# Three moves of small work in a fused attention and feed-forward kernel: a weight rounding, a square, and a group's last SiLU

## The chip, the cores and the metric

The kernel runs on one core of one Trainium2 chip. The metric is the device time of one execution in microseconds. TensorE (PE) does the matrix products, ScalarE (ACT) activations and copies, VectorE (DVE) elementwise work and reductions, GpSimd (POOL) elementwise work, and SyncE (SP) issues nearly all DMAs in program order.

## The reference, cut to what matters

Eight batches of twelve heads, 448 positions, head width 64. q and k are RMS-normalised, attention is a plain softmax, and its output, with heads side by side (3584 tokens of 768), goes through two matrix products with a SiLU between them. All is float32.

```python
scores = scale * np.matmul(rmsnorm(q, g_q), rmsnorm(k, g_k).transpose(0, 1, 3, 2))
attn = softmax(scores)                     # the scores' maximum is taken off first
x = np.matmul(attn, v)                     # -> (3584, 768)
h = x @ w_in                               # (768, 2048)
out = (h * (1.0 / (1.0 + np.exp(-h)))) @ w_out
```

The first three lines are shortened in notation, not in what they compute.

## The kernel before

**Couples and groups.** Attention is done in 24 couples of four heads, c = 0 to 23. Six couples (`GROUP`) are two batches. The first product of the feed-forward part, x @ w_in, is done for two batches at a time as eight blocks of seven products each (a Strassen scheme, class `Seven`), so the blocks of batches 0 and 1 run while couples 6 to 11 are attended, and so on. After the last couple the remaining blocks and the second product follow alone.

**A couple's two stretches.** `visit(c)` is the attention of couple c: pairs of score products go into the two PSUM buffers named `sc` (L749), ACT takes their exponentials (L754), and products with v add up in the two banks `av` (L786). `between(c)` runs the feed-forward products (L955, banks `mm` and `sc`) in two halves, by `fill`, which deals other small work among PE's steps, one piece after so many steps. What a piece issues goes into each engine's queue at that point of the program. The whole order is thus written out by hand: there is no scheduler, and each engine works its queue in order.

**The one-column write.** A visit first completes the sums of couple c-1 with its leftover keys. PE adds to the two `av` banks, and between two parts of that a single column of one bank is written by another engine (`turn`, L762: ACT up to couple 6, DVE at that place after it). PE's next product into that bank waits for it.

**The squares of q.** For couples up to 6, `normalise(c + 1)` gives pieces; piece 0 squares half of the next couple's q on ACT (L474) and reduces on DVE (L475). In visits 1 to 5 it is called by `run_all(beside[0:1])` ahead of the leftover products and of `turn`.

**Rounding of w_in.** The weights arrive as float64 words and are turned into float32 by pieces of 128x512: `open` is two ACT instructions (L103, L104), `round` three on DVE (L126, L129, L133) and an integer add on POOL (L137), and then issues the next loads (L88). Letters say where this is done: "o" opens, "r" rounds the next piece, in `halves` by half couple (index 2(c-6)+half) and in `visits` by visit; the first letter of a visit is done right behind its first scores.

```python
    halves = {0: "ro", 1: "ro", 2: "ro", 3: "oro", 4: "or", 5: "or", 6: "or", 7: "oroo"}
    visits = {GROUP + 2: "rr", GROUP + 4: "rr"}
```

**The SiLU.** `halves_in` runs the eight blocks of a group. A block's two finished rows of 128x896 are `owed`: their SiLU on ACT (L1102) and their save to `hidden` on SP (L994) are issued when the next block has finished its first product. The rows come from a ring of three (`staged`), so a block's second row is the row that the block before filled first; the copy of product 5 (L975) writes it. The last block of a group has no next one, and its rows are activated at once, at the end of couples 11, 17 and 23. ACT needs another function table for SiLU than for the exponential, and the kernel asks for the exponential's table ahead of each visit by a one-element activation (L1638).

**Later in a half.** The second half of a couple also holds, for couples from 7 on: the reciprocals of the row sums (L833), the transposition of the next k (L685) and its gain (ACT L691), the square of the q after next (L698), its reduction (L704) and a small product of that (L715), which is the last of PE's work ahead of the next visit.

Of the kernel before, what the change touches and what calls it, by code (L numbers as in the profile page):

```python
# [542 lines left out]
def bounded(  # L543
# [4 lines left out]
    HW, HF = z.NW // 2, z.NF // 2  # L548
# [5 lines left out]
    NC, loads, place, norm, spare, ones, first, squares = (  # L554
        own[name] for name in ("NC", "loads", "place", "norm", "spare", "ones", "first", "squares")
    )
    GROUP, LATE = z.NPAIR, z.LATE
# [12 lines left out]
    work = mem.tile([P, 16 * S + z.NK], F32, name="work")  # L570
    at = 0

    def piece(n):
        nonlocal at
        at += n
        return work[:, at - n : at]
# [5 lines left out]
    r = [piece(S) for _ in range(2)]  # L582
# [13 lines left out]
    for i, words in enumerate(late):  # L596
        m = len(pieces) - 4 + i
# [161 lines left out]
    def turn(step, copy):  # L759

        if step != weighed["step"]:
            copy(banks[1][:, S : S + 1], minus_half)  # L762
# [226 lines left out]
    def staged():  # L989
        stages.append(stages.pop(0))  # L990
        return stages[-1]

    def save(f, column, t):
        nc.sync.dma_start(hidden[f, :, ds(column, t.shape[1])], t)  # L994
# [11 lines left out]
    def fetch_ahead(group, m):  # L1006
        rows = [staged(), extra_stage if m else staged()]
        nc.sync.dma_start(rows[0], ahead[m])
        return rows, part_in(group, m, rows)
# [22 lines left out]
    def sum_x(group, c, steps=range(4)):  # L1032
        right_sums(*quarters(group, c), *sums_of_x(c), steps)

    def part_in(group, m, rows, prompt=False):

        chunk = 2 * m // room.CHUNK
        assert room.w_in.rounded >= (chunk + 1) * z.NW
        s = room.sums(chunk).rearrange("p (s c m k) -> p s c m k", s=3, c=HW, m=2)[:, :, :, m % 2]
        lefts = {  # L1040
            "1": lambda c: room.w1(c, 2 * m),
            "2": lambda c: room.w1(c + HW, 2 * m),
            "3": lambda c: s[:, 2, c],
            "4": lambda c: room.w1(c + HW, 2 * m + 1),
            "5": lambda c: s[:, 0, c],
            "6": lambda c: s[:, 1, c],
            "7": lambda c: room.w1(c, 2 * m + 1),
        }

        def right(name, c):  # L1050
            b11, b12, b21, b22 = quarters(group, c)
            t1, t2, t4 = sums_of_x(c)
            return {"1": b11, "2": b21, "3": b22, "4": t4, "5": t1, "6": t2, "7": b12}[name]

        def left(name, c):
            step = {"5": 0, "6": 1, "7": 2, "3": 3}.get(name)
            assert step is None or (chunk, step) in summed
            return lefts[name](c)

        done = {(i + 1, j + 1): rows[i][:, ts(j, S)] for i in range(2) for j in range(2)}  # L1060
        return Seven(left, right, range(HW), S, done, prompt)

    def halves_in(group, blocks, beside=lambda m: iter(()), begun={}, fetched=()):

        owed, ready = [], {}

        def prepare(m):
            if m in begun:
                return begun[m]
            if m in fetched:  # L1070
                return fetch_ahead(group, m)
            rows = [staged() for _ in range(2)]
            return rows, part_in(group, m, rows)

        for i, m in enumerate(blocks):
            rows, part = ready.pop(m) if m in ready else prepare(m)
            columns = part.five()
            if m not in begun and m not in fetched:
                columns = chain(part.two(), columns)
            aside = beside(m)  # L1080
            count = 0
            for n in columns:
                if n == 0:
                    yield n
                    continue
                count += 1
                if (count - 1) % HW == 0:
                    if count > HW:
                        activate(owed)
                    if count > 2 * HW and i + 1 < len(blocks) and blocks[i + 1] in fetched:  # L1090
                        if blocks[i + 1] not in ready:
                            ready[blocks[i + 1]] = prepare(blocks[i + 1])
                    next(aside, None)
                yield n
            for _ in aside:
                pass
            owed = [(2 * m + k, group[0], rows[k]) for k in range(2)]
        activate(owed)

    def activate(owed):  # L1100
        for f, b, t in owed:
            nc.scalar.activation(t, t, AF.Silu)  # L1102
            save(f, b * S, t)
        owed.clear()
# [144 lines left out]
    owed = []  # L1249
# [188 lines left out]


    step_of = {"o": lambda: room.w_in.open(), "r": lambda: room.w_in.round()}  # L1440
    halves = {0: "ro", 1: "ro", 2: "ro", 3: "oro", 4: "or", 5: "or", 6: "or", 7: "oroo"}
    visits = {GROUP + 2: "rr", GROUP + 4: "rr"}
    for c in range(GROUP // 2):
        halves[2 * (c - GROUP)], halves[2 * (c - GROUP) + 1] = "rr", "o"
    halves[-2], halves[-1] = "r", ""
# [21 lines left out]
    def last_two(c):  # L1467
        return [c // GROUP * 2 - 2, c // GROUP * 2 - 1]

    def visit(c):  # L1470

        beside = normalise(c + 1) if 0 < c <= GROUP else []
        if c == GROUP:
            beside = [lambda: None] + beside[2:]
        if c < NC:
            scores(c, 0, 0)
        for step in visits.get(c, "")[:1]:
            step_of[step]()
        if c == 0:
            first_q(1)  # L1480
            normalise_alone(1)
            scores(c, 1, 0)
        run_all(beside[0:1])
        if c > 0:
            weigh(c - 1, LEFT)
            weigh(c - 1, LEFT - 1, 0)
            turn(1, nc.scalar.copy if c <= GROUP else nc.vector.tensor_copy)
            if GROUP < c < NC and c % GROUP == 0:
                sum_x(last_two(c), 0, range(2, 4))
        if c < NC:  # L1490
            scores(c, 0, 1)
        if c > 0:
            weigh(c - 1, LEFT - 1, 1)
            if c - 1 < EARLY:
                for i in range(2):
                    nc.vector.tensor_copy(x_of(c - 1, i), sums[i])
                run_all(beside[1:2])
                if c == GROUP // 2 + 1:
                    divide(c - 2, None)
                if inverting:  # L1500
                    while len(inverting) > 1:
                        inverting.pop(0)()
                    if c > 1:
                        divide(c - 2, None)
            else:
                divide(c - 1, sums)
                if c == GROUP:
                    for i in range(1, HW):
                        sum_x(last_two(c), i, range(2))
                    for i in range(2):  # L1510
                        norm.scale(c + 1, q_of(c + 1), q_of(c + 1), i, nc.vector)
                    room.w_in.round()
                run_all(beside[1:2])
                if GROUP < c < NC and c % GROUP == 0:
                    for i in range(1, HW):
                        sum_x(last_two(c), i)
                weights_in_visit(c)
            if c + 1 < NC:
                loads["vrest"](c + 1)
        if c == NC:  # L1520
            return
        if c > 0:
            scores(c, 1, 0)
        scores(c, 1, 1)
        if c <= GROUP:
            run_all(beside[2:3])
        weigh(c, 0, 1)
        scores(c, 2, 0)
        weigh(c, 1, 1)
        turn(0, nc.scalar.copy)  # L1530
        if c < GROUP:
            run_all(beside[3:4])
        scores(c, 2, 1)
        weigh(c, 0, 0)
        if c < GROUP:
            scores(c, LEFT)
        if c != GROUP - 1:
            run_all(add(c, 1))
        weigh(c, 1, 0)
        if c < GROUP // 2:  # L1540
            room.w_in.open()
        if c >= GROUP:
            scores(c, LEFT)
        if c + 1 < NC:
            loads["v"](c + 1)
        if len(inverting) == 1:
            inverting.pop()()

    def run_all(work):
        for piece in work:  # L1550
            piece()

    def between(c):
# [36 lines left out]
        if c >= GROUP and c % GROUP == 0:  # L1590
            fetched = range(AHEAD) if c == GROUP else ()
            columns = products - 2 * HW * S * len(fetched)
            work = halves_in(last_two(c), range(HF), plain_in, dict(begun), fetched)
            begin(work, columns, 2 * GROUP)
            begun.clear()
        late = add(c, LEFT - 1) if c >= GROUP else []
# [46 lines left out]
    begun, inverting = {}, []  # L1643
# [23 lines left out]
    group = [z.B - 2, z.B - 1]  # L1667
# [219 lines left out]
```

## Time and profile before

| | us |
|---|---|
| median of 3 runs | 1303.18 (1303.07 to 1303.73) |
| the profiled execution's own time | 1303.14 |
| its span, first to last instruction | 1301.3 |
| PE busy in the span | 1289.3 |
| DVE busy | 955.8 |
| ACT busy | 503.7 |
| POOL busy | 357.1 |

The profile has one execution. Its parts are: busy time by engine, waits by pair of engine and releaser, and a timeline by engine with start, length, instruction and, in brackets, the idle time before it and what ended that. PE's matmuls are pipelined and their ends are modelled, so a late PE is read from its starts: a group of float32 products of 448 columns starts every 0.376 us when nothing holds it (two such groups, written x8 for the 64-row products, take 0.75 us). A visit's stretch from its first score product to the first feed-forward product behind it takes 10.97 us from 345.14 to 356.11, in couple 13.

### The profile page before, as it was taken

How to read it: one execution, taken by the hardware profiler on the slowest of the kernel's cores; microseconds unless marked ns; L12 is line 12 of the kernel's file. 1: busy time of each engine (PE TensorE's matmuls, PEld its weight loads, DVE VectorE, ACT ScalarE, POOL GpSimd, SP SyncE). 2: the span in 40 equal slices, each digit the busy share in tenths (PEclk: the TensorE clock that was granted, in tenths of full speed). 3: DMA queues.
4: the chain of work that ended last, by engine and by line, in shares of the span. 5: the costliest groups of instructions: out<-in, count | busy, mean ns of one | idle time of the engine just before them, and what ended most of it. 6: DMA issues, size and time to landing. Idle time of an engine off the chain costs nothing.

```text
span 1301.3 us, 19847 instructions
## 1 busy us (share of the span) xinstructions
PE 1289.3 (99%) x7182; PEld 831.3 (64%) x7182; DVE 955.8 (73%) x1650; ACT 503.7 (39%) x880; POOL 357.1 (27%) x221
## 2 busy tenths in 40 slices
PE   9999999999999999999999999999999999999998
PEld 4444444444444444444444455559999999999998
DVE  6998778868655557656554786698978787878785
ACT  7867566645554545544543344310000010000000
POOL 6755453443334334333311343400000000000000
PEclk9999999999999999999999999999999999999999
DMA  9674446434333444344321467312322223131411
GB/s 234 171 193 134 107 123 165 121 91 123 90 90 90 121 93 121 90 91 90 89 69 41 161 189 239 117 61 85 105 89 92 90 89 122 57 129 51 140 39 40
DMA packets 266159, 144.14 MB, mean 111 GB/s; under 512 B 203748, under 2 KB 249956, under 8 KB 266052
## 3 DMA queue, kind: packets, MB, share of 16 engines
q1 hardware_dynamic: 265424, 141.68, 39.5%
q8 instruction: 59, 0.97, 0.3%
q0 software_dynamic: 320, 0.90, 0.2%
q14 instruction: 48, 0.39, 0.1%
q10 hardware_dynamic: 308, 0.20, 0.1%
HBM read 95.36 MB, written 41.29 MB: 105 GB/s over the span
## 4 chain that ended last, share of the span: by engine, by line
PE 94%; ACT 2%; DVE 2%; issue 1%; DMA 0%; SPq 0%; POOL 0%; ACTq 0%; DVEq 0%; POOLq 0%
PE alone L1271 23%; PE mm L955 19%; PE sc L955 11%; PE av L786 10%; PE sc L749 10%; PE mm L1271 8%; PE alone L955 7%; PE alone L1309 2%; PE sc L824 1%; PE mm L824 1%; PE mm L1309 1%; PE sc L642 1%; PE sc L673 0%; DMA rows<-in_k_dram 0%; ACT work L754 0%
## 5 line engine op out<-in xcount | busy, mean ns | idle before, releaser
L754 ACT ACTIVATE work<-sc,rms 128x448 f32<-128x448 f32 x318 | 181.5, 634 | 74.2 <-PE sc L749 64.5
L749 PE MATMUL sc<-work 64*64 64x448 f32 x1344 | 164.3, 543 | 2.1 <-ACT work L754 0.9
L800 DVE TENSOR_TENSOR work<-work 128x896 f32<-128x896 f32 (+1 forms) x110 | 117.7, 1099 | 51.4 <-PE av L786 50.9
L786 PE MATMUL av<-work,rows 64*64 64x448 f32 x1272 | 151.3, 541 | 0.8 <-ACT av L762 0.5
L955 PE MATMUL mm<-x,W 128*128 128x448 f32 x366 | 150.2, 543 | 0.2 <-DVE stage L904 0.2
L955 PE MATMUL mm<-sums_x,W 128*128 128x448 f32 x348 | 143.2, 543 | 0.9 <-DVE stage L904 0.9
L503 POOL TENSOR_TENSOR rms<-rms,minus_half 128x14 f32<-128x14 f32 (+4 forms) x40 | 96.4, 2413 | 134.6 <-DVE rms L499 130.9
L530 POOL DMA_DIRECT2D out_dram<-x x2 | 1.2, 592 | 443.2 <-DVE x L904 443.2
L955 PEld LDWEIGHTS mm<-x,W 128*128 128x128 f32 x366 | 68.1, 190 | 72.3 <-issue 67.5
L1271 PE MATMUL alone<-W,rows 128*128 128x192 f32 x610 | 113.0, 326 | 0.0
L955 PEld LDWEIGHTS mm<-sums_x,W 128*128 128x128 f32 x348 | 64.9, 190 | 70.0 <-issue 64.8
L786 PEld LDWEIGHTS av<-work,rows 64*64 64x64 f32 x1272 | 58.3, 132 | 69.3 <-issue 33.4
L1271 PEld LDWEIGHTS alone<-W,rows 128*128 128x128 f32 x610 | 101.5, 190 | 0.0
L955 PE MATMUL sc<-x,W 128*128 128x448 f32 x246 | 100.1, 543 | 0.0
L749 PEld LDWEIGHTS sc<-work 64*64 64x64 f32 x1344 | 53.9, 132 | 70.7 <-ACT work L754 28.3
L719 POOL TENSOR_TENSOR rms<-rms,minus_half 128x28 f32<-128x28 f32 x15 | 72.1, 4806 | 64.9 <-DVE rms L716 64.9
L978 POOL TENSOR_TENSOR parts<-parts,stage 128x448 f32<-128x448 f32 x31 | 42.3, 1363 | 152.7 <-DVE parts L904 152.2
L955 PEld LDWEIGHTS sc<-x,W 128*128 128x128 f32 x246 | 46.0, 190 | 48.9 <-issue 45.4
L1271 PE MATMUL alone<-W,work 128*128 128x192 f32 x382 | 72.2, 326 | 0.0
L1102 ACT ACTIVATE stage<-stage 128x896 f32<-128x896 f32 x63 | 57.2, 944 | 22.1 <-DVE stage L904 21.4
L1281 ACT COPY rows<-alone 128x192 f32<-128x192 f32 x33 | 10.5, 317 | 141.6 <-PE alone L1271 141.6
L1271 PEld LDWEIGHTS alone<-W,work 128*128 128x128 f32 x382 | 63.8, 190 | 0.0
(265 smaller groups left out, 2292.6 us busy)
## 6 DMA issues: line engine op xcount, KB each, us to landing
hidden<-stage SPq DMA_DIRECT2D x63, 448.0 KB, 2.8
work<-hidden SPq DMA_DIRECT2D x21, 1024.0 KB, 5.1
rows<-in_moe_w_out_dram SPq DMA_DIRECT2D x32, 384.0 KB, 3.3
W<-in_moe_w_in_dram SPq DMA_DIRECT2D x22, 512.0 KB, 5.2
x<-hidden SPq DMA_DIRECT2D x7, 1024.0 KB, 5.7
rows<-in_q_dram SPq DMA_DIRECT2D x120, 56.0 KB, 2.2
rows<-in_k_dram SPq DMA_DIRECT2D x120, 56.0 KB, 2.3
rows<-in_k_dram SPq DMA_DIRECT2D x60, 96.0 KB, 2.6
```

The costliest lines, as they stand in the source:

```text
L503: nc.gpsimd.tensor_tensor(out=t, in0=t, in1=half, op=ALU.pow)
L719: nc.gpsimd.tensor_tensor(out=f, in0=f, in1=minus_half.to_broadcast([P, n]), op=ALU.pow)
L749: nc.tensor.matmul(two[ds(half * D, D), h, 0:S], keys[rows, ts(half, D)], qT[rows, pair, :], start=True, stop=True,)
L754: nc.scalar.activation(left_weights(c)[:, h] if j == LEFT else weights(c, j)[:, i, h], two[:, h, 0:S], AF.Exp, scale=norm.column(c, i, h, j),)
L786: nc.tensor.matmul(sums[i][ds(h * D, D), :], v, w, start=(j == 0 and step == 1), stop=(j == LEFT - 1 and step == 1),)
L800: nc.vector.tensor_tensor(out=total, in0=total, in1=more, op=ALU.add)
L824: nc.tensor.matmul(t[ds(h * D + i * n, n), :], ones[:, which + i if which else 0], left_weights(c)[:, h] if which else w()[:, i, h], start ...
L955: nc.tensor.matmul(t, self.left(name, s), self.right(name, s), start=s == ends[0], stop=s == ends[1])
L978: nc.gpsimd.tensor_tensor(out=u2, in0=u2, in1=p5, op=ALU.add)
L1102: nc.scalar.activation(t, t, AF.Silu)
L1271: nc.tensor.matmul(t, x[:, i], y, start=i == ORDER[0], stop=i == ORDER[-1])
L1309: nc.tensor.matmul(o, a[:, 2 * i + m, t], right_one(name, i)[:, m], start=n == 0, stop=n == len(steps) - 1,)
```

## The change

Three edits. (1) `halves` and `visits`: the opening of one piece moves from the first half of couple 9 to the second half of couple 8, and its rounding from the first half of couple 9 to the head of visit 9; the last opening of the second half of couple 9 finds no piece left. (2) In visits 1 to 5 the first squaring of q comes behind the leftover products and `turn`. (3) A group's last two owed rows are handed to the next group's `halves_in` where there is a next one (couples 11 and 17), which issues their SiLU and save when its own first product is done.

```diff
+    carried = []
-    def halves_in(group, blocks, beside=lambda m: iter(()), begun={}, fetched=()):
+    def halves_in(group, blocks, beside=lambda m: iter(()), begun={}, fetched=(), carry=False):
-        owed, ready = [], {}
+        owed, ready = list(carried), {}
+        carried.clear()
...
             owed = [(2 * m + k, group[0], rows[k]) for k in range(2)]
-        activate(owed)
+        if carry:
+            carried.extend(owed)
+        else:
+            activate(owed)
...
-    halves = {0: "ro", 1: "ro", 2: "ro", 3: "oro", 4: "or", 5: "or", 6: "or", 7: "oroo"}
-    visits = {GROUP + 2: "rr", GROUP + 4: "rr"}
+    halves = {0: "ro", 1: "ro", 2: "ro", 3: "oro", 4: "or", 5: "oor", 6: "o", 7: "oroo"}
+    visits = {GROUP + 2: "rr", GROUP + 3: "r", GROUP + 4: "rr"}
...
-        run_all(beside[0:1])
-        if c > 0:
+        if c == 0:
+            run_all(beside[0:1])
+        else:
             weigh(c - 1, LEFT)
             weigh(c - 1, LEFT - 1, 0)
             turn(1, nc.scalar.copy if c <= GROUP else nc.vector.tensor_copy)
+            run_all(beside[0:1])
...
-            work = halves_in(last_two(c), range(HF), plain_in, dict(begun), fetched)
+            work = halves_in(last_two(c), range(HF), plain_in, dict(begun), fetched, c + GROUP < NC)
```

## The prediction, made before the changed kernel ran

> **What bounds the kernel now.** First the page's busy times.
>
> ```profile
> PE 1289.3 (99%) x7182; PEld 831.3 (64%) x7182; DVE 955.8 (73%) x1650; ACT 503.7 (39%) x880; POOL 357.1 (27%) x221
> ```
>
> PE sets the time, so a change that gives PE no fewer products can only remove PE's waits. Second, PE's waits (who waited, for whom: us, times, longest):
>
> ```profile
> PE mm L955 <- DVE stage L904: 1.0, 2, 0.9
> PE sc L749 <- ACT work L754: 0.9, 3, 0.4
> PE av L786 <- ACT av L762: 0.5, 2, 0.2
> PE sc L749 <- ACT work L691: 0.5, 1, 0.5
> ```
>
> These idle times understate a wait, since the modelled ends reach into it. So I went third to the timelines of PE and ACT at each place and read starts. Visit 1:
>
> ```profile
> 26.31 0.93 PE L749 MATMUL sc<-work 64*64 64x448 f32 x8
> 27.47 0.98 PE L786 MATMUL av<-work,rows 64*64 64x448 f32 x8 [0.23 <-ACT av L762]
> 25.70 1.13 ACT L754 ACTIVATE x<-sc,rms 128x448 f32<-128x448 f32 x2
> 26.73 0.62 ACT L474 ACTIVATE rows<-x 112x512 f32<-112x512 f32 x1
> 27.25 0.16 ACT L762 COPY av<-minus_half 128x1 f32<-128x1 f32 x1
> ```
>
> The av products were due at 26.31 + 0.75 = 27.06 and came 0.41 late; the square stands ahead of the column write. The same reading gives 0.42 in visit 4 (due 76.64, came 77.06), 0.15 in visit 5, nothing in visits 2 and 3. Visit 12, the first of a new group:
>
> ```profile
> 315.33 2.03 PE L749 MATMUL sc<-work 64*64 64x448 f32 x16 [0.26 <-ACT work L754]
> 311.77 0.95 ACT L1102 ACTIVATE stage<-stage 128x896 f32<-128x896 f32 x1 [0.76 <-DVE stage L904]
> 312.74 1.28 ACT L1638 ACT_TABLE_LOAD   x1
> 314.14 3.45 ACT L754 ACTIVATE work<-sc,rms 128x448 f32<-128x448 f32 x6
> 345.14:356.11 10.97, 10.97 (x113) 4.92 (x113) 2.83 (x6) 8.88 (x16) 6.49 (x2) 1.00 0.42 122
> 311.08:322.68 11.60, 11.27 (x114) 4.01 (x113) 10.54 (x18) 9.12 (x16) 6.96 (x2) 1.00 0.51 132
> ```
>
> The scores began at 311.08, but ACT, held by the last SiLU and the table load, started its exponentials at 314.14. The last two lines, busy times by window (stretch, its length, PE first), show the price: 11.60 us against 10.97 for an undisturbed visit. Visit 18 has 11.54 (512.40 to 523.94). Last, the end of couple 9:
>
> ```profile
> 243.99 1.77 PE L955 MATMUL mm<-sums_x,W 128*128 128x448 f32 x4 [0.85 <-DVE stage L904]
> 245.60 0.30 PE L715 MATMUL sc<-rms,ident 128*128 128x28 f32 x2
> 246.37 0.98 PE L749 MATMUL sc<-work 64*64 64x448 f32 x8 [0.47 <-ACT work L691]
> 243.32 0.93 ACT L698 ACTIVATE rows<-rows 128x896 f32<-128x896 f32 x1
> 244.16 0.66 ACT L103 ACTIVATE W<-W 128x512 int32<-128x512 uint32 x1
> 245.29 1.02 ACT L691 ACTIVATE work<-work,gains 128x896 f32<-128x896 f32 x1
> 243.35 0.58 DVE L904 TENSOR_TENSOR stage<-mm,stage 128x448 f32<-128x448 f32 x1
> 244.28 1.09 DVE L704 TENSOR_REDUCE rms<-rows 128x28 f32<-128x896 f32 x1 [0.35 <-ACT rows L698]
> ```
>
> PE's product before began at 240.72; six groups later, at 242.98, the next was due, and came 1.01 late, because DVE read its bank at 243.35. Then L749 came 0.77 behind L715, where couple 11 has 0.23 (310.85 to 311.08): 0.54 more, for the gain L691, which stood behind an opening (L103, L104).
>
> **What the Trainium skill says.** "Perfetto Trace Analysis", Per-engine timelines: ACT and DVE are strict first-in-first-out, and PE's end is estimated; the trace agrees, as L762 follows L474 though its data were there. "ScalarE: Activation LUTs", What ACT_TABLE_LOAD costs: about 1283 ns, plus a drain of about 1380 ns; here the load takes 1.28 us, and the activation starts 0.01 us behind it, without that drain. "GPSIMD Engine Reference", Key points: GpSimd shares SBUF interfaces with VectorE; here L129 took 1.24 us at 231.81 beside a POOL sum, and 0.43 at 241.25. "Perfetto Trace Analysis", DMA Instruction — HWDGE: the final semaphore write can be late when the target is HBM; the saves L994 land 2.5 to 5.8 us after issue, median 2.8.
>
> **The change part by part.**
>
> *Rounding.* Couple 9 loses 0.42 + 1.24 + 1.50 = 3.2 us of DVE at 231.35 and the opening of 1.2 us at 244.16. I follow the queue: L904 goes at 233.1, when its product is done; L475, the second square and L475 follow to 235.6; the reciprocal starts at 235.7 instead of 236.97; the chain behind it, 6.4 us to L904 at 243.35, ends near 242.7. The bank is free by 242.9, so the 1.01 goes. What is late next: L715 needs L704, which needs the square L698, and ACT's order up to L698 is unchanged and hangs on a PE product ending at 238.63. So L704 still ends at 245.37, L715 starts at 245.42, L749 at 245.65. Gain 246.37 - 245.65 = 0.72; bounds 0.3 (L704 a little later) and 1.55 (L698 comes forward as well).
> Where the work lands: the opening goes into ACT's idle 3.74 us ahead of 209.15. Its words land at 206.75, so it runs 206.8 to 208.1 and the square L698 to 209.0, which leaves L691 at 209.15 where it was. The rounding in visit 9 begins behind L716 (213.34); in visit 10 the same three end 1.71 us after L716's start, here 215.05, and the column write behind them started at 215.33, having waited 1.81 for PE: hidden, with 0.28 to spare, and past that PE pays one for one. POOL's add follows the power L719 near 218.4 and may slow DVE by up to 1.1 (L129's 1.24, L133's 1.50); DVE has its 0.66 idle at 230.8 and the 3.2 removed. On SP two loads of 0.4 move ahead of the v loads (216.85), which nobody needs before the next couple, and from ahead of the k loads (230.78), which gain it. Cost nothing.
>
> *Squares.* In visit 1 ACT is free at 26.73, the write is done at 26.89, PE continues at 27.06. The square then ends where write and square ended before, so the exponentials still start at 27.36; fourth scores due at 28.56 find their bank free at 28.56, the fifth (due 30.07) find it at 30.13. That late start and PE's restart cost 0.1 in each of the three visits. But a restart of 0.05 at the old stall also goes: 0.36 + 0.38 + 0.08 = 0.82; bounds 0.3 and 0.98. In visits 2 and 3 the write waits for PE (42.51, 58.12) and the square ends before the next scores: nothing. DVE's reduction moves by up to 0.5, with av copies that PE needs 0.5 later.
>
> *SiLU.* ACT is free for the table after L691 (308.66), so the exponentials follow the scores, as in couple 13. Gain 11.60 - 10.98 and 11.54 - 10.98 (10.97 to 10.99 in other visits): 1.18; bounds 0.9 and 1.2. In couple 12 a table load and two SiLUs, 1.28 + 1.79 = 3.1 us, go behind the first product's copy (325.24) into an idle 5.70 us; the load that stood at 342.66 falls away, so none is added. The save goes behind eight q loads on SP (325.41 + 3.98 = 329.4; SiLU done at 328.2, so the queue does not stop) and ahead of the k loads. L975, at 332.00 before, writes that row and must wait for the landing: with 3.0 us (the save at 428.91 stands in the same order and took 3.03) it starts at 332.5. Behind it stand the second square, L475 and the reciprocals, whose end is 5.17 us later (0.43 + 0.56 + 0.68 + 1.96 + 1.54) and frees the buffer PE wants at 339.0. So L975 may be as late as 333.8, a landing of 4.4 us. Hidden.
>
> *Sum.* 0.72 + 0.82 + 1.18 = 2.72, from 1303.14: 1300.42. The median shown is 0.04 higher, so 1300.5.
>
> **Rivals.** (a) New waits take more: rounding 0.5, squares 0.3, SiLU 1.18 together 2.0, 1301.2. For it: ACT has almost no slack in visits 1 to 5. Against: visits 2 and 3 run the same queue without the stall. (b) More comes: 1.55 + 0.98 + 1.2 = 3.7, 1299.5. For it: earlier DVE may relieve what I can't see. Against: L698's order. (c) Slower: the carried save. If it lands past 4.4 us, PE pays one for one in couples 12 and 18; the gain of 2.7 is gone at 1.35 past that, 5.8 us, which is the longest landing seen, and at 7.1 the kernel is slower by 0.2%: 1305.8. Against: couple 15 saves in this order with no PE wait. That the change doesn't do what it says is ruled out: the built kernel's queues show the copy ahead of the square, the SiLU carried, the rounding moved, and PE's order untouched.
>
> **How the numbers follow.** 0.2% is 2.6 us, about what a measurement of this kernel can tell from no change; the line is 1300.57. Forecast 0.60 (1299.9 to 1301.0, two thirds of it below the line), (a) 0.17, (b) 0.18, (c) 0.05. Faster: 0.40 + 0.18 = 0.58. Slower by over 0.2%: 0.03 of (c). Same: the rest, 0.39. The range 1299.4 to 1301.8 takes in (a) and nearly all of (b).
>
> **What would show it.** Right: visits 12 and 18 last 11.0; visit 1's av products start 0.75 behind the scores; in couple 9 PE waits once, at L715, for L704. Wrong: a wait of L975 on a save that reaches PE, a column write of visit 9 behind L133, or L749 waiting for exponentials in visits 1, 4 and 5.

## The result and the profile after

The changed kernel takes 1300.77 us (median of 21 runs, 1300.35 to 1302.07), the kernel before 1303.36 beside it (21 runs, 1303.04 to 1304.85): 2.59 us less, a ratio of 0.998 with a 95% interval of 0.9973 to 0.9986. The profiled execution took 1300.95 us, its span is 1299.1. Line numbers of the changed kernel are up to eight higher: L1102 is L1108, L1638 is L1646.

The page's busy times first, then the two lines of PE's waits (us, times, longest) that answer to those shown of the kernel before.

```profile
PE 1288.5 (99%) x7182; PEld 833.8 (64%) x7182; DVE 952.4 (73%) x1650; ACT 504.0 (39%) x880; POOL 358.4 (28%) x221
```

```profile
PE sc L715 <- DVE rms L704: 0.6, 1, 0.6
PE sc L749 <- ACT work L754: 0.4, 1, 0.4
```

The wait for L904 in couple 9 is no longer in the list (what is left of that line is 0.2 us in couple 7), the waits for L762 on ACT and for L691 are gone, and the wait for L754 went from three to the one at the start of the kernel. One wait is new in the places that the change touches: PE at L715. (Another, 0.4 us at L673 for a load of k, stands at the start of this execution.) The timelines of PE and ACT in visit 1 (start, length, engine, line, and in brackets the idle time before and what ended it):

```profile
26.44 0.93 PE L749 MATMUL sc<-work 64*64 64x448 f32 x8
27.19 0.93 PE L786 MATMUL av<-work,rows 64*64 64x448 f32 x8
26.84 0.18 ACT L762 COPY av<-minus_half 128x1 f32<-128x1 f32 x1
26.92 0.65 ACT L474 ACTIVATE rows<-x 112x512 f32<-112x512 f32 x1
```

The write now stands ahead of the square, and the av products start 0.75 behind the scores. The visit takes 11.23 us, from 24.13 to 35.36; before it took 11.57. Visit 4 went from 11.59 to 11.23, visit 5 from 11.39 to 11.40. Couple 12, first the window of visit 12 (stretch, its length, then the busy time of PE, PEld (PE's weight loads), DVE, ACT and POOL, the granted clock, which is the share of TensorE's full clock that it was given, the DMA share and GB/s), then ACT and SP (SPq is SP issuing a DMA):

```profile
309.95:320.97 11.02, 11.02 (x113) 5.00 (x112) 9.97 (x17) 6.90 (x13) 6.96 (x2) 1.00 0.31 56
```

```profile
311.03 1.16 ACT L754 ACTIVATE work<-sc,rms 128x448 f32<-128x448 f32 x2 [1.99 <-PE sc L749]
324.08 1.28 ACT L1108 ACT_TABLE_LOAD   x1
331.26 0.53 ACT L975 COPY stage<-mm 128x448 f32<-128x448 f32 x1 [3.57 <-DMA hidden<-stage]
328.36 0.90 SPq L994 DMA_DIRECT2D hidden<-stage  x2
```

The exponentials start 1.08 us behind the scores (309.95), where they were 3.06 behind before; the table load and the SiLU pair stand behind the first product. L975 waits for the save, and nobody waits for L975: from visit 12's end to visit 13 it is 22.47 us, as before. The end of couple 9, PE, ACT and DVE:

```profile
240.16 4.14 PE L955 MATMUL mm<-sums_x,W 128*128 128x448 f32 x10
244.90 0.41 PE L715 MATMUL sc<-rms,ident 128*128 128x28 f32 x2 [0.60 <-DVE rms L704]
245.24 0.98 PE L749 MATMUL sc<-work 64*64 64x448 f32 x8
242.79 0.93 ACT L698 ACTIVATE rows<-rows 128x896 f32<-128x896 f32 x1
243.63 1.03 ACT L691 ACTIVATE work<-work,gains 128x896 f32<-128x896 f32 x1
243.76 1.09 DVE L704 TENSOR_REDUCE rms<-rows 128x28 f32<-128x896 f32 x1 [1.28 <-ACT rows L698]
```

Ten product groups now run on with 0.2 us lost (4.14 us; undisturbed they would take nine starts of 0.376 and a last group of 0.54, 3.92), where before PE came 1.0 us late in the middle of them. Then PE stops at L715, for L704, for L698, which ends at 243.72 behind the table load and the SiLU pair. From visit 9's end to visit 10 it is 22.05 us, before 22.62.

The trace's gains by place: 0.34 and 0.36 in visits 1 and 4, -0.01 in visit 5, 0.57 in couple 9, 0.57 each in visits 12 (11.59 to 11.02) and 18 (11.54 to 10.97), together 2.40 us. This execution began 0.12 us later than that of before (first scores at 9.45 instead of 9.33, behind that load of k) and lost 0.08 in the part after the last couple, so its own gain is 2.19; the medians say 2.59, and their interval, 1.8 to 3.5 us, covers both. The runs of the kernel before that were made beside the experiments below have medians of 1303.12 to 1303.22, not 1303.36; against these the changed kernel's median would gain 2.35 to 2.45, close to the trace's sum.

### The profile page after: what moved, and what is told of

The parts are those of the page before. It is cut to its first block, busy times and chain, and to the rows that moved or that the text cites. A ratio compares the mean times of both kernels' runs of the same rounds, so it can differ in the third digit from the quotient of the medians.

```text
span 1299.1 us, 19842 instructions
## 1 busy us (share of the span) xinstructions
PE 1288.5 (99%) x7182; PEld 833.8 (64%) x7182; DVE 952.4 (73%) x1650; ACT 504.0 (39%) x880; POOL 358.4 (28%) x221
## 4 chain that ended last, share of the span: by engine, by line
PE 96%; DVE 2%; ACT 1%; DMA 1%; issue 0%; POOL 0%; SPq 0%; ACTq 0%; DVEq 0%; POOLq 0%
PE alone L1277 23%; PE mm L955 20%; PE sc L955 11%; PE av L786 10%; PE sc L749 10%; PE mm L1277 8%; PE alone L955 7%; PE alone L1315 2%; PE sc L824 1%; PE mm L824 1%; PE mm L1315 1%; PE sc L642 1%; PE sc L673 0%; DVE work L904 0%; DVE work L800 0%
## 5 line engine op out<-in xcount | busy, mean ns | idle before, releaser
L754 ACT ACTIVATE work<-sc,rms 128x448 f32<-128x448 f32 x318 | 181.9, 635 | 84.7 <-PE sc L749 72.6
L749 PE MATMUL sc<-work 64*64 64x448 f32 x1344 | 165.0, 543 | 1.2 <-ACT work L652 0.7
L749 PEld LDWEIGHTS sc<-work 64*64 64x64 f32 x1344 | 54.9, 132 | 68.0 <-ACT work L754 26.0
L978 POOL TENSOR_TENSOR parts<-parts,stage 128x448 f32<-128x448 f32 x31 | 43.1, 1389 | 151.1 <-DVE parts L904 150.2
L1108 ACT ACTIVATE stage<-stage 128x896 f32<-128x896 f32 x63 | 57.0, 945 | 17.7 <-DVE stage L904 17.1
```

The costliest lines, as they stand in the source:

```text
L749: nc.tensor.matmul(two[ds(half * D, D), h, 0:S], keys[rows, ts(half, D)], qT[rows, pair, :], start=True, stop=True,)
L754: nc.scalar.activation(left_weights(c)[:, h] if j == LEFT else weights(c, j)[:, i, h], two[:, h, 0:S], AF.Exp, scale=norm.column(c, i, h, j),)
L978: nc.gpsimd.tensor_tensor(out=u2, in0=u2, in1=p5, op=ALU.add)
```

## The experiments

Differences of half a microsecond are at the edge of what the times tell, so each kernel is judged by its stretch in the trace, and by its median as support. Medians are set against the runs of the kernel before made beside them.

| kernel | median, us | against before, us | ratio, 95% | stretch that it tests, us |
|---|---|---|---|---|
| changed | 1300.77 | -2.59 | 0.9973 to 0.9986 | visit 9's end to visit 10: 22.05 (before 22.62) |
| opening_alone | 1302.65 | -0.57 | 0.9986 to 1.0003 | the same: 22.09 |
| rounding_late_opening | 1303.20 | -0.02 | 0.999 to 1.0007 | the same: 22.64 |
| squares_alone | 1302.58 | -0.64 | 0.9986 to 1.0002 | visits 1 and 4: both 11.23 |
| silu_alone | 1302.10 | -1.12 | 0.9984 to 0.9997 | visits 12 and 18: 11.02, 10.97 |
| square_early | 1299.96 | -3.25 | 0.9965 to 0.9984 | visit 9's end to visit 10: 21.18 |
| square_early_rounding_back | 1300.94 | -2.27 | 0.9975 to 0.999 | the same: 22.09 |
| clamps_visit9 | 1301.30 | -1.91 | 0.9978 to 0.9992 | visit 9: 11.28 (changed 10.97) |
| clamps4_visit9 | 1302.12 | -1.00 | 0.9986 to 1.0003 | visit 9: 12.20 |
| save_late | 1301.49 | -1.72 | 0.998 to 0.9993 | couples 12, 18: 22.81, 22.83 (changed 22.47) |
| save_six | 1303.28 | +0.10 | 0.9991 to 1.0009 | the same: 23.74, 23.76 |
| save_later | 1307.84 | +4.72 | 1.0023 to 1.0048 | the same: 26.38, 26.41 |

**The opening alone.** The changed couple 9 mixes two moves, an opening on ACT and a rounding on DVE. The first kernel makes only the opening's.

```diff
-    halves = {..., 4: "or", 5: "or", 6: "or", 7: "oroo"}
+    halves = {..., 4: "or", 5: "oor", 6: "ro", 7: "oroo"}
```

> The kernel before with only the opening moved: one opening more in the second half of couple 8, the one ahead of the gain L691 in couple 9 gone; the rounding stays in the first half of couple 9. Theory (couple 9 waits twice in a row, and each of the two edits can take only its own wait): the wait for the bank, 1.0 us, stays, and the 0.54 us for L691 goes; the stretch from visit 9's end to visit 10's first scores 22.62 -> 22.08 us, kernel -0.5 us. Rival (the bank's 1.0 us is what the change gained, the opening is incidental): the stretch stays at 22.6 us, kernel 0.0 us.

PE's timeline of that kernel at the end of couple 9:

```profile
244.00 1.77 PE L955 MATMUL mm<-sums_x,W 128*128 128x448 f32 x4 [0.86 <-DVE stage L904]
245.61 0.30 PE L715 MATMUL sc<-rms,ident 128*128 128x28 f32 x2
245.84 0.98 PE L749 MATMUL sc<-work 64*64 64x448 f32 x8
```

The wait for L904 is all there (244.00, as before at 243.99), L715 follows unhindered, and L749 comes at its usual 0.23 behind it instead of 0.77. The gain is 0.53 us, of the 0.57 that both moves bring.

**The rounding moved, the late opening kept.** The other half. The last letter "a" opens the last piece a second time, in the place of the late opening.

```diff
-    halves = {..., 4: "or", 5: "or", 6: "or", 7: "oroo"}
-    visits = {GROUP + 2: "rr", GROUP + 4: "rr"}
+    halves = {..., 4: "or", 5: "oor", 6: "o", 7: "oroa"}
+    visits = {GROUP + 2: "rr", GROUP + 3: "r", GROUP + 4: "rr"}
```

> The kernel before with the rounding and the opening moved as in the change, but the late opening ahead of L691 kept, by opening the last piece a second time (it writes the same values again). Theory: the bank is free in time, and the 1.0 us comes back whole at the scores, which wait for L691 behind the opening: ACT's order up to there hangs on a product that ends at 238.6, so the stretch stays within 0.1 of 22.62 us and the kernel within 0.1 us. Rival (DVE's rounding was the cost): the stretch is 22.0 us, kernel -0.6 us.

Its timeline, PE and ACT:

```profile
245.44 0.41 PE L715 MATMUL sc<-rms,ident 128*128 128x28 f32 x2 [0.59 <-DVE rms L704]
246.37 0.98 PE L749 MATMUL sc<-work 64*64 64x448 f32 x8 [0.52 <-ACT work L691]
245.29 1.03 ACT L691 ACTIVATE work<-work,gains 128x896 f32<-128x896 f32 x1
```

DVE is early, all but 0.2 us of the bank's wait is gone, and it helps nothing: L691 ends where it ended, and L749 starts at 246.37, to the hundredth where it started before. So in the changed kernel the opening's move earns 0.53 us and the rounding's, added to it, 0.04; alone the rounding's earns nothing (22.64 against 22.62).

**The squares alone, and the SiLU alone.**

```diff
-        run_all(beside[0:1])
-        if c > 0:
+        if c == 0:
+            run_all(beside[0:1])
+        else:
             weigh(c - 1, LEFT)
             weigh(c - 1, LEFT - 1, 0)
             turn(1, ...)
+            run_all(beside[0:1])
```

> The kernel before with only the squares behind the column write in visits 1 to 5. Theory: visit 1 takes 11.23 us (11.57 before), visit 4 11.23 (11.59), visits 2, 3 and 5 are unchanged within 0.03; kernel -0.70 us. Rival (part of the gain in those visits came from the two other edits, or visit 5 loses what 1 and 4 win): under 0.5 us.

Visits 1 to 5 take 11.23, 11.25, 11.22, 11.23 and 11.40 us (11.57, 11.25, 11.22, 11.59, 11.39 before): 0.34 and 0.36 in visits 1 and 4, and nothing in the others.

For the SiLU, the changed kernel with the two other edits taken back.

> The kernel before with only the carried SiLU pair. Theory: visits 12 and 18 take 11.02 and 10.97 us (11.59 and 11.54), couples 12 and 18 themselves are unchanged, kernel -1.14 us; with the two other parts alone, -0.57 and -0.70, the sum is -2.4 us, so the parts add up. Rival (the carried save costs part of it back in couples 12 and 18): the stretch from visit 12's end to visit 13 is over 22.5 us, and the kernel gains under 0.9 us.

Visits 12 and 18 take 11.02 and 10.97, and the stretches behind them 22.47 as before. The parts add up: by stretches 0.57 + 0.69 + 1.14 = 2.40, where the 0.57 of couple 9 is the changed kernel's own, since its two moves together were not run alone.

**The square of couple 9 early.** What is left there should be L698 alone.

```diff
             turning = prompt[2:3] + [lambda: square(c + 2)]
+            if c == LATE:
+                turning.pop()
+                first_of_two = prompt[1]
+                prompt[1] = lambda: run_all([first_of_two, lambda: square(c + 2)])
             prompt[2:3] = [lambda: run_all(turning)]
```

> The changed kernel with the square L698 of couple 9 issued some eight products earlier, ahead of the copy L966 instead of behind the SiLU pair. Theory (what is left in couple 9, 0.76 us of PE at L715 and a late restart, is the square alone, standing behind a table load and two SiLUs): L704 finds its rows ready and runs right behind L904, L691 comes up by one square to 242.8, L715 starts unhindered at 244.14, L749 at 244.37 instead of 245.24; the stretch from visit 9's end to visit 10 is 21.2 us instead of 22.05, kernel -0.87 us against the changed one (-3.4 against the one before). Rival (the next wait stands right behind, at L691 or at the exponential's table): under 0.4 us.

PE and ACT of that kernel:

```profile
243.99 0.30 PE L715 MATMUL sc<-rms,ident 128*128 128x28 f32 x2
244.22 0.98 PE L749 MATMUL sc<-work 64*64 64x448 f32 x8
242.63 1.03 ACT L691 ACTIVATE work<-work,gains 128x896 f32<-128x896 f32 x1
```

PE runs through from L715 to the scores; the stretch is 21.18 us, 0.87 less than with the changed kernel, as expected. At 1299.96 us this is the fastest of all, 0.81 under the changed kernel.

**The same with the rounding back in couple 9.**

```diff
-    halves = {..., 5: "oor", 6: "o", 7: "oroo"}
-    visits = {GROUP + 2: "rr", GROUP + 3: "r", GROUP + 4: "rr"}
+    halves = {..., 5: "oor", 6: "ro", 7: "oroo"}
+    visits = {GROUP + 2: "rr", GROUP + 4: "rr"}
```

> The kernel of square_early with the rounding back in the first half of couple 9 (the opening stays moved). Theory (the two waits of couple 9 lie one behind the other, so the move of the rounding earns nothing while the square is late, and its full wait once the square is early): the bank's wait of 1.0 us is back, the stretch is 22.1 us as with the changed kernel, and the kernel is 0.9 us slower than square_early and level with the changed one within 0.1. Rival (the rounding's move is worth nothing in either order): level with square_early.

The stretch is back at 22.09, with PE's product at 245.00 waiting 0.86 for L904. (Its profiled execution also lost 1.3 us in visit 4, 12.51 instead of 11.22, most of it in a wait of PE for a DVE copy, and 0.3 behind it; its other runs lie at 1300.7 to 1301.6.) So the rounding's move is worth 0.04 us with the square late, and 0.91 with the square early. The gain of the pair is not the sum of its parts, because PE reaches its scores only when DVE's and ACT's chains are both done.

**How much visit 9 can hide.** The prediction gave the rounding at the visit's head 0.28 us to spare. Two more copies of its first instruction use that up.

```diff
+            for _ in range(2 * self.again):      # 1 at the head of visit 9, else 0
+                nc.vector.tensor_scalar(out=dst, in0=dst, scalar1=HIGH_MIN, ...)
```

> The changed kernel with the first rounding instruction of visit 9 (L126) repeated twice, 0.92 us more of DVE at the head of that visit, same values. The column write behind it had 0.29 us to spare. Theory (past that, PE pays one for one): the write is 0.63 us late, visit 9 lasts 11.6 us instead of 10.97, kernel +0.6 us against the changed one. Rival (the scores and products behind make up for it, or more waits follow): visit 9 under 11.2 or over 11.9 us.

The column write (here L768) and the products behind it (here L792), from the timelines of DVE and PE:

```profile
215.33 0.15 DVE L768 COPY av<-minus_half 128x1 f32<-128x1 f32 x1
215.54 0.98 PE L792 MATMUL av<-work,rows 64*64 64x448 f32 x8
```

In the changed kernel the write ran at 214.77 and the products at 215.28. The write is 0.56 later, the products only 0.26, and the visit lasts 0.31 longer. Both expectations missed: the write had ended at 214.93, 0.35 ahead of the products that need it, and that is a second reserve behind the 0.29 that the bracket shows. Four copies then test the slope.

> As clamps_visit9, with four repeats of the clamp instead of two: another 0.92 us of DVE at the head of visit 9. Two repeats cost visit 9 only 0.31 us, 11.28 instead of 10.97, where 0.63 had been expected. Theory (the slack is not 0.28 but 0.6 us, since the column write also ended 0.35 us ahead of the product that needs it; past it one for one): visit 9 lasts 12.2 us. Rival (PE makes up part of any delay in the visit): under 11.9 us.

Visit 9 takes 12.20 us: 0.92 more of DVE, 0.92 more of PE.

**The carried save late.** The prediction's slow rival: the row's landing comes so late that PE waits. Small loads ahead of the saves on SP make it late.

```diff
             nc.scalar.activation(t, t, AF.Silu)
+            while late_saves:                     # 4, 6 or 8 of them, once in couples 12 and 18
+                i = late_saves.pop()
+                nc.sync.dma_start(waste[:, i : i + 1], own["keys"][0, 0, 0:P, i : i + 1])
             save(f, b * S, t)
```

> The changed kernel with four small loads, of 128 values each into a buffer that nobody reads, on SP ahead of the carried saves in couples 12 and 18. Each takes SP some 0.4 to 0.5 us, so the first save is issued 1.6 to 2.0 us later, at 330.0 to 330.4, and L975, which writes its row again, starts at 332.9 to 333.3 instead of 331.26; the limit worked out in the prediction is 332.1 in this kernel's time. Theory (past the limit PE pays one for one): PE waits 0.8 to 1.2 us in each of the two couples, their stretches are 23.3 to 23.7 us instead of 22.47, kernel +1.6 to +2.4 us against the changed one. Rival (the chain behind L975 has more slack than its 5.2 us suggest): stretches 22.5 us, kernel within 0.2 us.

L975 (here L976) ran at 332.76. PE was due at the product that waits at 337.80 and came 0.26 late:

```profile
338.06 2.49 PE L956 MATMUL sc<-x,W 128*128 128x448 f32 x6
```

The stretches are 0.34 and 0.36 us longer, not 0.8 to 1.2. The limit is real, but some 0.6 us later than the expectation had it, and that is a slip in carrying it over from one kernel's time to another's. The prediction's limit, 333.8, stands in the time of before (as the profile of the kernel before counts it), where visit 12 starts at 311.08: it is 22.72 us behind that start. The changed kernel starts visit 12 at 309.95, so its limit is 332.67. The expectation took off 1.7 us, the shift behind visit 12, and so counted the 0.57 us that visit 12 gains a second time. Here visit 12 starts at 309.80 and L975 22.96 us later, 0.24 past 22.72, and PE is 0.26 late: the prediction's limit holds. From L975's start to the end of the second reciprocal it was 5.15 us (332.76 to 337.91), where the prediction had 5.17.

> As save_late, with eight loads instead of four ahead of the carried saves: another 1.9 us (four took 1.94). With four, L975 was 1.66 us later than in the changed kernel and PE lost 0.34 and 0.36 us in couples 12 and 18, so the limit lies 1.3 us past the changed kernel's L975. Theory (past the limit one for one): stretches of couples 12 and 18 of 24.7 us instead of 22.8, kernel +4.5 us against the changed one, 1305.3, so slower than the kernel before: the price at which the third rival would have decided. Rival (the wait also holds back something else, or other work fills in): stretches over 25.2 or under 24.2 us.

The stretches are 26.4 us, not 24.7; that is in the rival's range, but not for the rival's reasons. PE's timeline and windows (stretch, length, PE busy, granted clock, DMA share, GB/s) in couple 12:

```profile
340.02 4.19 PE L956 MATMUL sc<-x,W 128*128 128x448 f32 x6 [1.98 <-DVE work L834]
```

```profile
341.00:342.00 1.00, 1.00 (x2) 0.50 0.23 61
```

PE comes 2.15 us late (due at 337.87), 1.9 more than with four loads, as one for one would have it. But then its six groups take 4.02 us up to the next, instead of 2.26: the granted clock stands at 0.5 and a group starts every 0.747 us instead of 0.376. That is 1.76 us more, in couple 18 too, and it accounts for all of the difference to what was expected. Six loads should then show the slope without the clock.

> As save_late and save_later, with six loads. With four PE was 0.26 us late at the product that waits, and the stretch 0.34 us longer; with eight it was 2.15 us late and the stretch 3.9 us longer, since the granted clock fell to 0.5 for 3.4 us behind the pause. Theory (one for one past the limit, and the rest is the clock's fall behind a pause of two microseconds): PE is 1.2 us late, the clock stays at 1.0, stretches of couples 12 and 18 of 23.75 us, kernel +2.5 us against the changed one, 1303.3. Rival (the rest comes with any pause there, or the clock falls at this length too): stretches of 25 us and more, kernel over 1305.

They do: stretches of 23.74 and 23.76, the clock at 1.00 around both pauses, 1303.28 us. PE came 1.19 us late to the product (due at 337.82):

```profile
339.01 2.49 PE L956 MATMUL sc<-x,W 128*128 128x448 f32 x6 [1.04 <-DVE work L834]
```

## Why the prediction was right

**The time.** 1300.5 was forecast, 1300.77 measured, inside the range of 1299.4 to 1301.8. The move of 2.59 us is 0.199%, just short of the 0.2% that the prediction drew between "faster" (chance 0.58) and "same" (0.39). By the trace's places the sum came out at 2.40 instead of 2.72: all three parts were forecast too large, the first by 0.15, the second by 0.13 and the third by 0.04.

**Rounding, 0.72 forecast, 0.57 measured.** The chain that ends last was right: L704 still waits for L698, L698 still hangs on the product before it, and PE's new wait is at L715. Two sizes were off. L715 began at 244.90, which is 245.46 in the time of before, 0.04 later than worked out; and L749 came 0.34 behind it, not 0.23. The 0.23 was read where PE runs through; behind the wait PE took up again some 0.1 us more slowly. A third step failed, and it cost nothing here. The bank was not free by 242.9, in time for PE: the L904 behind the rounding's old place was to go at 233.1 "when its product is done", and went at 233.59 in the time of before,

```profile
233.03 0.62 DVE L904 TENSOR_TENSOR stage<-mm,parts 128x448 f32<-128x448 f32 x1 [1.03 <-POOL parts L978]
```

because it also needs a sum of POOL's (L978), which took 1.97 us where it took 1.18 before. That leaves the 0.2 us in the ten groups, which vanish in the longer wait at L715. What the prediction didn't see is whose gain it was: it followed DVE's queue for most of its working, and the runs give nearly all of it to the opening that left ACT's queue.

**Where that work lands.** In couple 8 the opening ran at 206.24 and L691 at 208.60, which is 206.80 and 209.16 in the time of before (0.56 us later there); 206.8 and 209.15 were forecast. In visit 9 the rounding is hidden, as forecast; its reserve is 0.6 us and not 0.28, for the idle time in front of the column write was counted and the time between its end and PE's need was not. POOL's add beside it slowed DVE about as far as the prediction allowed for (L728 took 2.18 us, 1.09 before), and no wait of PE came of it.

**Squares, 0.82 forecast, 0.69 measured.** Visits 1 and 4 gave 0.34 and 0.36 (forecast 0.36 and 0.38), visits 2 and 3 nothing, as forecast. The 0.08 of visit 5 failed: the write there now waits for PE itself (0.62 us), PE's next product still comes at 96.81, 0.08 late behind one that started at 95.98, and what that saves of the 0.15 is lost again in the scores behind it (from 97.61 to the next av products 1.61 us, before 1.51). The prediction had set 0.1 for this late start in each of the three visits. (Its own terms, 0.41, 0.42 and 0.15 less a net 0.05 each, give 0.36, 0.37 and 0.10; the sum is the same within 0.01.)

**SiLU, 1.18 forecast, 1.14 measured.** The visits last 11.02 and 10.97. Counted from visit 12's start, which is 1.13 us earlier in the changed kernel, the save was issued at 329.49 in the time of before (328.36; forecast 329.4) and landed in 2.80 instead of 3.0, and L975 ran at 332.39 (331.26; forecast 332.5), and was hidden.

**Rival (c).** Its mechanism is shown by the three kernels with loads ahead of the save, and its limit was right. In these, L975 ran at 332.76, 333.72 and 334.72, visit 12 starts at 309.80, 309.82 and 309.88, and PE came 0.26, 1.19 and 2.15 us late. That puts the limit 22.70, 22.71 and 22.69 us behind visit 12's start; 333.8 is 22.72 behind it. (The product that wants the bank stands at 339.65 in the trace of before; less the 0.57 that visit 12 gains this is 339.08, the 339.0 of the prediction.) Past the limit the stretch grew one for one, with some 0.1 us on top, up to a wait of 1.19 us; at 2.15 us it grew by 3.9. So the price that (c) gave a far later save was too low: it had 1305.8 us for 2.7 us past the limit, and the median at 2.15 was 1307.84. In the changed kernel 1.4 us are left: L975 runs at 331.26, and the limit is 332.65. Rival (b), that L698 comes forward as well, didn't happen by itself; square_early shows what it was worth, 0.87.

## What to carry to other kernels

Where two queues each hold up the same product, ask of every move on one queue what the other will allow: here the rounding's move was worth 0.04 us or 0.91, depending on where a square stood on another engine. Cover has two parts, the idle time in front of an instruction and the time between its end and the need of whoever waits for it, and only both together gave the limit that the runs showed. A limit worked out in one kernel's times is carried over to another kernel's by the shift between the two just ahead of the place where the change gains; with the shift behind that place, the gain counts twice. A PE pause that is twice as long can cost more than twice as much: 1.27 us for one of 1.19, 3.9 for one of 2.15 behind which the clock fell.

## What the runs showed of the hardware

A pause of PE of 2.15 us brought the granted clock down to 0.5 for some 3.4 us and cost 1.76 us beyond itself, in both couples of the profiled execution of save_later (0.08 of it the slow restart, which the pause of 1.19 us cost too). The fall did not come with the pause but behind it. PE had taken up again at 340.02 and 544.66, and the windows from there (stretch, length, PE busy, granted clock, DMA share, GB/s)

```profile
340.00:341.00 1.00, 0.98 (x2) 0.70 0.00 0
544.60:546.50 1.90, 1.84 (x3) 0.66 0.03 7
```

have these means if the clock went from 1.0 to 0.5 at 340.40 and 545.21, some 0.4 and 0.55 us later. Pauses of 0.26 and 1.19 us in the same places left it at 1.00. The Trainium skill, "TensorE: Matmul & The Clock Gate", Part 1: The HAM clock gate, puts the fall to half clock behind an idle window of about 3.4 us that runs freely; here it came with a pause of 2.15, too short to fill such a window, and the measurement decides. How long a pause has to be, between 1.19 and 2.15 us, and whether it also depends on when it falls, was not tested.

The six runs of that kernel lie at 1306.9 to 1307.1 and at 1308.6 to 1308.8, three each. Their mean granted clocks are on record: 0.998 in each of the faster three, 0.996 in each of the slower, the profiled one among them, and one fall is worth 0.0013 of the mean (half of 3.4 us in 1307). The times fit too: by an estimate from 1300.77 us and the stretches above, two pauses make 1305.2 us with no fall, 1306.9 with one and 1308.6 with two. So in the faster three most likely only one of the two pauses met a fall, and a pause of this length brings it often, but not always. Which of the two it was stays open, since only one execution was profiled.
